# One rewrite of a two-branch kernel: u per column quarter, angle multiples by ScalarE's scale, sums in place, copies on two engines, a new written order

## The chip, the core and the metric

The kernel runs on one core of a Trainium2 chip. The core has five engines that run their own instruction streams side by side: TensorE (PE in the profile; its weight loads are shown as PEld), VectorE (DVE), ScalarE (ACT), GpSimd (POOL) and SyncE (SP), which here issues transfers. On-chip memory is SBUF (128 partitions) and PSUM, eight banks of 512 fp32 numbers per partition, into which TensorE writes. The metric is the device time of one execution in microseconds. Three runs of the kernel before gave 300.64, 302.02 and 304.17 us; the median is 302.02 us.

## What is computed

Two independent branches, of which the outputs stand side by side in the last dimension (448 + 448 columns, bf16, 2048 rows).

```python
# branch A: linear attention, 16 heads of 28, softmax feature maps
q, k, v = split(x @ wqkv)                           # x is 2048 x 448
phi(t)  = concat(softmax(t @ w_phi), softmax(-t @ w_phi))
kv, z   = phi(k)^T v, sum(phi(k))                   # per head, over all 2048 rows
o       = (phi(q) @ kv) / (phi(q) . z + 1e-6)
a       = o @ wo
# branch B: a state space layer as a long convolution, 448 channels, 256 complex states
P[d,n,l] = exp(dt[d] * A[d,n] * l)                  # l = 0..2047
K[d,l]   = Re sum_n C[d,n] * P[d,n,l] * dt[d] * B[d,n]
y        = irfft(rfft(pad(u)) * rfft(pad(K)))[:2048]
b        = y + u * Dskip
```

## The kernel before

**Branch A.** Weights are folded with `w_phi` on TensorE (`fold_weights`), x is transposed on TensorE (`flip_x`, L379), then `key_side` (L600 and around it) walks over eight pairs of row blocks: projections on TensorE, two Exp per block on ScalarE, a DMA transpose, a reciprocal (L187) and a scaled product on VectorE, and an accumulation in two PSUM banks. `query_side` does four chunks of 512 rows: projections, Exp, normalisation on VectorE, one small round trip through DRAM (`SCd`) to spread the scales over partitions, and the output projection.

**Branch B, the kernel K.** The 448 channels are done in four column quarters of 112 channels. A power P at l is split into a low factor (48 positions, tile `W`) and a high factor (16 positions, tile `U`). Per quarter, ScalarE makes the low factor's parts: `rotations` (cosine and sine of 16 multiples of an angle, tile `T`) and `dampings` (Exp of 31 multiples of a decay). In this kernel the odd multiples of angle and decay come from TensorE: `args` multiplies the high and low bf16 halves of `TH` or `AT` by identities scaled by 1, 3, ..., 15 (`PID`), four multiples to two PSUM banks, and one ScalarE instruction then covers up to four multiples, times 1, 2, 4, 8 or 16 by its scale:

```python
items += acc(psum[:, bs[e // 2], at:at + QC], [(PID[:, 4 * grp + e, :], src[:, part, cols]) for part in range(2)])
```

That is 12 ScalarE instructions for the rotations and 11 for the dampings of a quarter. VectorE multiplies the two (`damp`), extends the low factor (`far` with its inner `step`) and makes the high factor by doubling (`hi_tables`; two tiles `U` take turns). `build_k` is 448 matmuls per quarter, 16 columns of `U` against 48 of `W`, with four ScalarE copies; `scatter_k` takes the result through DRAM (`KTd`) to another layout. Since `W` is one tile, `damp` of the next quarter waits until `build_k` has read it.

**Branch B, the convolution.** It is done by matmuls with cosine tables in two halves of 1024 rows. `signal_spectrum` transforms all of u for both halves (128 matmuls of 448 columns, 16 copies on ScalarE) and writes it to DRAM (`SUd`); `conv_loads` reads it back per quarter. `kernel_spectrum_pair` transforms K of the first two quarters together, `kernel_spectrum` of each of the last two, with tables of 384 KB for each of eight frequency blocks (`load_f`, 16 transfers in all; the last two quarters share one set, held in SBUF). `conv` of a quarter is VectorE's three products of 3584 columns, one sum, one product with `Dskip`, ten smaller sums (`finish`), and 144 matmuls (`inverse`), with four copies on ScalarE and four output transfers.

**Order.** All operations are recorded in a list (`Prog.add`, L94) and issued in an order written out by hand as numbers (`ORDER`, L845); the PSUM banks are written out too (`SLOTS`). Each engine runs its own instructions strictly in that order. Nearly all VectorE work has line L162 (`tt`), ScalarE's functions have L190 (`af`), its copies L193 (`acopy`), matmuls L201, transposes L211, and transfers L216 on SP or POOL. The quarter names used below count from (0) to (3). In this order `conv` of the first quarter begins after the tables of the fourth, so that all four convolutions stand at the end.

Of the kernel before, what the change touches and what calls it, by code (L numbers as in the profile page):

```python
# [13 lines left out]
AX = mybir.AxisListType  # L14
PI = float(np.pi)

D_MODEL = 448
# [7 lines left out]
ODD = list(range(1, 16, 2))  # L25
# [9 lines left out]
SPLIT = [[(0, QC)]] * 3 + [[(0, 112), (112, 112)]]  # L35

def _round_bf16(a):
    import ml_dtypes
    return np.asarray(a, np.float32).astype(ml_dtypes.bfloat16)

# [6 lines left out]
def _dft_tables():  # L47
    m = np.arange(512) ^ 64
# [4 lines left out]
    GO = G[:, :, :, np.arange(512) ^ 64]  # L53
    GI = np.stack([GO, GO[:, :, :, ::-1]])
# [17 lines left out]
    pid = np.zeros((128, 9, 128))  # L72
    for i, p in enumerate(ODD + [-1]):
        pid[np.arange(128), i, np.arange(128)] = p
# [6 lines left out]
    return tuple(_round_bf16(t) for t in (G, GI, FT, pid, hm, hz))  # L81

class Prog:

# [9 lines left out]
    def add(self, eng, fn):  # L94
        self.ops.append((eng, fn))

    def issue(self, i):
        self.ops[i][1]()

    def run(self, order):  # L100
        assert sorted(order) == list(range(len(self.ops)))
        for i in order:
            self.issue(i)

@with_exitstack
def kernel(
# [19 lines left out]
    consts = _dft_tables()  # L126
    G_d, GI_d, F_d, P_d, M_d, Z_d = (nc.inline_tensor(t, name=f"const{i}").ap() for i, t in enumerate(consts))
    dram = ctx.enter_context(tc.tile_pool(name="dram", bufs=1, space=bass.MemoryType.DRAM))
    SUd = dram.tile([4, 128, 8, D_MODEL], BF16, name="SUd")
# [62 lines left out]
    def acopy(o, a):  # L192
        prog.add("A", lambda: nc.scalar.copy(o, a))  # L193

# [19 lines left out]
    def dma(eng, o, i):  # L214
        e = {"S": nc.sync, "AD": nc.scalar, "G": nc.gpsimd}[eng]
        prog.add(eng, lambda: e.dma_start(out=o, in_=i))  # L216

    oCB, oAT, oTH, oPW, oW, oT, oU, oTM, oSQ, oTS, oKT, oX = (
        3584, 7168, 10752, 14336, 95104, 32256, 46592, 75264, 82432, 86912, 92400, 139008)
    PID = sb(0, [128, 9, 128])  # L220
    ident = PID[:, 0, :]
    NEG = PID[:, 8, :]
    DSK = sb(2304, [128, D_MODEL])
    HM = sb(3200, [112, 4, D_HEAD + 1])
    K0 = sb(86016, [128, D_MODEL])
    bias_hp = sb(3440, [128, 1], F32)
    KVZ = sb(3456, [112, 2, 4, 4, 2])
    CB = sb(oCB, [128, 2, NCOL])
    AT = sb(oAT, [128, 2, NCOL])
    TH = sb(oTH, [128, 2, NCOL])  # L230
    PW = {k: sb(oPW + 3584 * i, [128, 2, NCOL]) for i, k in enumerate((32, 64, 128, 256, 512))}
    W = sb(oW, [128, 2, N_LO, QC])
    T = sb(oT, [128, 2, 16, QC])
    U = [sb(oU + 14336 * b, [128, N_HI, 2, QC]) for b in range(2)]
    TS = [sb(oTS + 2744 * b, [128, N_LO, 28]) for b in range(2)]
    KT = [sb(oKT + 1344 * b, [128, N_KT, 112]) for b in range(2)]

    prog.add("V", lambda: nc.vector.memset(psum[:, 4:8, 0:7 * N_LO], 0.0))
    prog.add("V", lambda: nc.vector.memset(psum[:, 0:4, 0:7 * N_LO], 0.0))
    xT = sb(oX, [112, 4, 2048])  # L240
    Wp = [sb(o, [112, 4, D_MODEL]) for o in (155392, 158976)]
    WV = sb(162560, [112, 4, D_MODEL])
    M = sb(158976, [112, 8, D_MODEL])
    wo = sb(166144, [112, 4, D_MODEL])
    G1 = sb(169728, [128, 2, 4, 512])
    raw = {nm: sb(oT + 2048 * i, [112, 4, SSM_N]) for i, nm in enumerate(("Are", "Aim", "Cre", "Bre", "Cim", "Bim"))}
    srcs = {"Are": B_A_re, "Aim": B_A_im, "Cre": B_C_re, "Bre": B_B_re, "Cim": B_C_im, "Bim": B_B_im}
    XS = [sb(o, [128, 4, D_MODEL]) for o in (oW + 10976, oW + 14560, oW + 18144, oW + 32928)]
    Wqk = sb(oW + 36512, [112, 4, 2 * D_MODEL])
    wT = sb(oTS, [112, 2, 4, D_MODEL])  # L250
    BD = sb(oTS + 7168, [112, 4, 112])
    DG = sb(oSQ + 1024, [112, 4, 112])
    DGN = sb(oSQ + 1920, [112, 4, 112])
    ldt = sb(oSQ + 2816, [4, 112])
    dtr = sb(oSQ + 3072, [4, 112])
# [10 lines left out]
    dma("S", PID, P_d)  # L266
    load_raw("Aim")
    load_x(0)
    for nm in ("Cre", "Bre", "Cim", "Bim"):
        load_raw(nm)  # L270
    for i in range(1, 4):
        load_x(i)
    dma("S", Wqk, wq3[:, :, 0:2 * D_MODEL])
    mset(BD, 0.0)
    for hh in range(4):
        dma("G", BD[28 * hh:28 * hh + 28, :, 28 * hh:28 * hh + 28], A_w_phi.rearrange("(c h) d f -> h d c f", h=4)[hh])
    prog.add("V", lambda: nc.vector.memset(bias_hp, PI / 2))

    def rep_rows(row, a):
        rs = u2.ap[0][0]  # L280
        return bass.AP(tensor=u2.tensor, offset=u2[row + 128 * (1 - a), 0].offset,
                       ap=[[2 * rs, 64], [256 * rs, 4], [1, D_MODEL]])

    def pair_rows(row, t):
        rs = u2.ap[0][0]
        return bass.AP(tensor=u2.tensor, offset=u2[row + 1023 - 128 - 256 * t, 0].offset,
                       ap=[[128 * rs, 2], [-2 * rs, 64], [1, D_MODEL]])

    ua = [sb(o, [128, 4, 2, D_MODEL]) for o in (oU, oW + 10976)]
    ab = [sb(o, [128, 2, 4, D_MODEL]) for o in (198336, oU + 14336)]  # L290

    def load_u(b):
        for a in range(2):
            dma("S", ua[b][64 * a:64 * a + 64, :, 0, :], rep_rows(1024 * b, a))
        for t in range(4):
            dma("G", ua[b][:, t, 1, :], pair_rows(1024 * b, t))

    load_u(0)
    dma("S", G1, G_d)
    dma("S", WV, wq3[:, :, 2 * D_MODEL:])  # L300

# [7 lines left out]
    def two(bs, parts=128):  # L309
        return view(psum[0:parts, bs[0], 0:1], [512 * (bs[1] - bs[0]), 2], [1, D_MODEL])  # L310
# [611 lines left out]
```

## Time and profile before

The profiled execution's span, from its first to its last instruction, is 299.6 us; the page gives no other time for that execution. The median of the three timed runs, 302.02 us, is 2.4 us above it.

| engine | busy us | share | instructions |
|---|---|---|---|
| PE matmul | 240.7 | 80% | 3877 |
| PEld | 179.8 | 60% | 3877 |
| DVE | 244.4 | 82% | 292 |
| ACT | 203.4 | 68% | 343 |
| POOL | 16.0 | 5% | 32 |

DMA moves 39.47 MB. A share of the span is a mean over stages; the stages are told apart by the windows view, which gives each engine's busy time in a stretch of the span, and by the groups of instructions kept apart by shape. An ACT instruction overlaps the one behind it, so that the busy time of a group is less than count times mean.

### The profile page before, as it was taken

How to read it: one execution, taken by the hardware profiler on the slowest of the kernel's cores; microseconds unless marked ns; L12 is line 12 of the kernel's file. 1: busy time of each engine (PE TensorE's matmuls, PEld its weight loads, DVE VectorE, ACT ScalarE, POOL GpSimd, SP SyncE). 2: the span in 40 equal slices, each digit the busy share in tenths (PEclk: the TensorE clock that was granted, in tenths of full speed). 3: DMA queues.
4: the chain of work that ended last, by engine and by line, in shares of the span. 5: the costliest groups of instructions: out<-in, count | busy, mean ns of one | idle time of the engine just before them, and what ended most of it. 6: DMA issues, size and time to landing. Idle time of an engine off the chain costs nothing. (4 is left out here: it accounts for less than half of the span.)

```text
span 299.6 us, 8829 instructions
## 1 busy us (share of the span) xinstructions
PE 240.7 (80%) x3877; PEld 179.8 (60%) x3877; DVE 244.4 (82%) x292; ACT 203.4 (68%) x343; POOL 16.0 (5%) x32
## 2 busy tenths in 40 slices
PE   1246997899469999986979996566998888999784
PEld 1245554567245567863447763466658678999784
DVE  4265995446249999997989999989899999999991
ACT  3749999599947999997199955871948611544431
POOL 8102201001000000000000001000000000000000
PEclk9999999999959999998695999777999999999999
DMA  7999387463804530045012533955879956667222
GB/s 161 239 231 194 79 246 145 64 181 67 107 10 122 122 64 4 6 136 104 3 61 58 85 79 85 331 146 109 227 255 293 301 136 176 147 184 135 46 65 63
DMA packets 65966, 39.47 MB, mean 132 GB/s; under 512 B 46616, under 2 KB 61992, under 8 KB 65544
## 3 DMA queue, kind: packets, MB, share of 16 engines
q1 hardware_dynamic: 62920, 31.57, 45.0%
q0 software_dynamic: 3008, 7.34, 8.9%
q8 instruction: 30, 0.49, 0.7%
q14 instruction: 8, 0.07, 0.1%
HBM read 26.36 MB, written 8.85 MB: 118 GB/s over the span
## 5 line engine op out<-in xcount | busy, mean ns | idle before, releaser
L201 PE MATMUL psum<-sbuf 128*16 128x48 bf16 (+9 forms) x3768 | 231.3, 258 | 39.1 <-DVE sbuf L162 11.1
L201 PEld LDWEIGHTS <-sbuf 128*16 128x16 bf16 (+4 forms) x3768 | 170.7, 109 | 98.3 <-issue 37.3
L162 DVE TENSOR_TENSOR sbuf<-sbuf 128x896 bf16<-128x896 bf16 (+13 forms) x227 | 216.7, 1002 | 12.1 <-DMA sbuf<-SCd 3.5
L193 ACT CAST sbuf<-psum 128x448 bf16<-128x448 f32 (+4 forms) x141 | 74.9, 581 | 70.6 <-PE psum L201 63.1
L190 ACT ACTIVATE sbuf<-psum 128x448 bf16<-128x448 f32 (+4 forms) x140 | 81.7, 674 | 13.2 <-DVE sbuf L162 7.5
L211 PE MATMUL psum<-sbuf 128*112 128x128 bf16 (+3 forms) x109 | 11.7, 267 | 16.2 <-DMA sbuf<-in_A_x_dram 7.2
L190 ACT ACTIVATE sbuf<-psum,sbuf 128x896 bf16<-128x896 f32 (+3 forms) x28 | 21.7, 812 | 0.0
L211 PEld LDWEIGHTS <-sbuf 128*112 128x112 bf16 (+3 forms) x109 | 10.0, 172 | 17.8 <-DMA sbuf<-in_A_x_dram 7.7
L187 DVE RECIPROCAL sbuf<-psum 128x64 bf16<-128x64 f32 x8 | 4.4, 555 | 19.4 <-PE psum L201 19.4
L190 ACT ACT_TABLE_LOAD x13 | 16.7, 1283 | 0.9 <-PEq L906 0.7
L190 ACT ACTIVATE sbuf<-sbuf 128x896 bf16<-128x896 bf16 (+3 forms) x13 | 11.6, 915 | 3.6 <-DVE sbuf L162 3.4
L180 DVE COPY sbuf<-psum 112x1024 bf16<-112x1024 bf16 (+2 forms) x16 | 7.3, 466 | 7.8 <-PE psum L211 6.6
L216 POOL DMA_DIRECT2D sbuf<-const x4 | 2.2, 556 | 126.0 <-PE psum L201 109.5
L162 DVE TENSOR_TENSOR sbuf<-psum,sbuf 128x128 f32<-128x128 f32 (+3 forms) x10 | 4.7, 491 | 3.8 <-ACT sbuf L193 3.8
L193 ACT COPY sbuf<-psum 112x896 bf16<-112x896 bf16 x5 | 4.5, 919 | 4.7 <-PE psum L211 4.7
L216 POOL DMA_DIRECT2D sbuf<-in_B_u_dram x8 | 6.6, 830 | 19.0 <-DMA sbuf<-in_B_B_re_dram 18.9
L174 DVE TENSOR_SCALAR sbuf<-sbuf 128x3584 bf16<-128x3584 bf16 (+4 forms) x11 | 6.5, 587 | 0.0
L216 POOL DMA_DIRECT2D sbuf<-SUd x4 | 2.1, 529 | 72.5 <-DVE sbuf L162 72.5
L193 ACT CAST sbuf<-sbuf 128x1792 bf16<-128x1792 f32 x3 | 5.1, 1703 | 0.0
L180 DVE COPY sbuf<-sbuf 128x448 bf16<-128x448 bf16 (+1 forms) x6 | 1.4, 238 | 3.1 <-DMA sbuf<-const 3.1
L177 DVE SCALAR_TENSOR_TENSOR sbuf<-sbuf 128x64 f32<-128x64 f32 (+1 forms) x6 | 3.0, 506 | 0.0
L196 POOL MEMSET sbuf<- 128x32 bf16 (+3 forms) x6 | 1.4, 261 | 24.7 <-PE psum L211 24.5
(12 smaller groups left out, 9.4 us busy)
## 6 DMA issues: line engine op xcount, KB each, us to landing
sbuf<-const SPq DMA_DIRECT2D x16, 384.0 KB, 3.2
SUd<-sbuf SPq DMA_DIRECT2D x8, 448.0 KB, 4.3
sbuf<-SCd SPq DMA_DIRECT2D x16, 224.0 KB
sbuf<-SUd POOLq DMA_DIRECT2D x4, 896.0 KB, 4.9
sbuf<-const POOLq DMA_DIRECT2D x2, 1024.0 KB, 7.9
sbuf<-in_A_x_dram SPq DMA_DIRECT2D x4, 448.0 KB
out_dram<-sbuf SPq DMA_DIRECT2D x4, 448.0 KB
sbuf<-in_B_u_dram SPq DMA_DIRECT2D x16, 112.0 KB, 4.0
```

Of the source, the lines that this page charges most:

```text
L162: prog.add("V", lambda: nc.vector.tensor_tensor(out=o, in0=a, in1=b, op=op))
L174: prog.add("V", lambda: nc.vector.tensor_scalar_mul(o, a, s))
L177: prog.add("V", lambda: nc.vector.scalar_tensor_tensor(out=o, in0=a, scalar=s, in1=b, op0=op0, op1=op1))
L180: prog.add("V", lambda: nc.vector.tensor_copy(o, a))
L187: prog.add("V", lambda: low(lambda: nc.vector.reciprocal(o, a)))
L190: prog.add("A", lambda: nc.scalar.activation(o, a, fn, **kw))
L193: prog.add("A", lambda: nc.scalar.copy(o, a))
L196: prog.add("G", lambda: nc.gpsimd.memset(o, v))
L201: nc.tensor.matmul(o, lhsT=l, rhs=r, **kw)
L211: nc.tensor.transpose(o, i, idn)
L216: prog.add(eng, lambda: e.dma_start(out=o, in_=i))
```

## The change

- **Angle and decay multiples.** `AT` and `TH` are kept as fp32 in SBUF; `args` and the scaled identities are gone. Each multiple is a ScalarE instruction of its own over 224 columns with the multiple as its scale: 32 per quarter for `rotations`, 31 for `dampings`.
- **u per quarter.** `signal_spectrum`, the loads of whole u and the round trip through `SUd` are gone. `u_rows` loads one quarter of u (two transfers of 224 KB), `u_spectrum` reverses the odd rows by a matmul, makes sum and difference on VectorE, transforms them (128 matmuls of 112 columns per quarter) and copies to SBUF; the product with `Dskip` is two instructions.
- **Kernel spectrum.** Each quarter for itself; the table tiles are loaded anew for each quarter (32 transfers of 384 KB) into three places.
- **Convolution.** `finish` writes its sums over the products' own tile: eight sums per quarter where there were ten.
- **Branch A.** Two row blocks share an Exp or a copy (896 or 1024 columns where there were 448 or 512).
- **Copies.** Each former copy can be on ScalarE or VectorE by a written table; 15 are on VectorE, among them four of the eight of `flip_x`, which were all there before.
- **Buffers.** One tile `U` and one `TS` (two before), a tile of its own for the dampings, two places for temporaries, two for products.
- **Order.** Written anew: the convolutions of the first two quarters stand before the end of the fourth quarter's tables, those of the last two after.

Instructions as built: TensorE 4261 matmuls and transposes and as many weight loads (3877 before), VectorE 297 (292 before), ScalarE 423 and 20 activation table loads (330 and 13 before).

```diff
-    def acopy(o, a):
-        prog.add("A", lambda: nc.scalar.copy(o, a))
+    def copy(o, a):
+        prog.either("A", lambda e: (nc.scalar.copy(o, a) if e == "A" else nc.vector.tensor_copy(o, a)))
...
+CLASSES = {
+    "T": [(117888, 7168), (125056, 7168)],
+    "C": [(137664, 7168), (144832, 7168)],
+    "F": [(166336 + 3072 * i, 3072) for i in range(3)],
+}
...
     def rotations(qt):
-        for grp in range(2):
-            p0, far_ = args(TH, qt, grp)
...
+        src = TH[:, qt * QC:(qt + 1) * QC]
+        for r, p in enumerate(LO_ABS):
+            af(T[:, 0, r, :], src, ACT.Sin, scale=float(p), bias=bias_hp)
+            af(T[:, 1, r, :], src, ACT.Sin, scale=float(p))

     def dampings(qt):
...
+        src = AT[:, qt * QC:(qt + 1) * QC]
+        for r in range(31):
+            af(A[:, r, :], src, ACT.Exp, scale=float(LO[r]))
...
+    def u_rows(qt):
+        for r in range(2):
+            dma("S", UA[qt][:, r].rearrange("p b t x -> p (b t) x"), ...)
+
+    def u_spectrum(qt):
+        ua, su, AB, RV = UA[qt], SU[qt], AB_[qt], RV_[qt]
+        bs = prog.take("P", 0, 1)
+        mms([(psum[:, bs[b], 0:D_MODEL], REV, ua[:, 1, b].rearrange("p t x -> p (t x)"), dict(start=True, stop=True))
+             for b in range(2)])
+        copy(RV.rearrange("p b t x -> p b (t x)"), two(bs))
+        add(AB[:, :, 0], ua[:, 0], RV[:, :, ::-1, :])
+        sub(AB[:, :, 1], ua[:, 0], RV[:, :, ::-1, :])
+        for b in range(2):
+            for cp in range(2):
+                bs = prog.take("P", *((0, 1), (2, 3))[cp])
+                for st in range(2):
+                    mms([it for mt in range(4) for it in acc(
+                        psum[:, bs[st], 112 * mt:112 * mt + 112],
+                        [(GS[0][:, cp, jt, 128 * mt:128 * mt + 128], AB[:, b, cp ^ st, jt, :]) for jt in range(4)])])
+                copy(su[:, b, cp].rearrange("p s m x -> p s (m x)"), two(bs))
...
+    def kernel_spectrum(qt):
+        sk, kt_ = SK[qt % 2], KT[qt % 2]
+        for mp in range(4):
+            fts = []
+            for k in range(2):
+                ft = sb(FP[prog.take("F", (2 * mp + k) % 3)[0]], [128, 2, 6, 128])
+                dma("S", ft, F_d[2 * mp + k])
...
         def finish(b, t):
-            y = Y[:, b]
+            y, S = t[:, 0], t[:, 1].rearrange("p r (c x) -> p r c x", c=2)
             sub(y[:, 0], t[:, 0, 0], t[:, 1, 1])
             add(y[:, 1], t[:, 0, 1], t[:, 1, 0])
-            S = S_[:, b]
             add(S[:, 0], y[:, :, 0:448], y[:, :, 448:896])
-            sub(S[:, 1, 0], y[:, 0, 0:448], y[:, 0, 448:896])
-            sub(S[:, 1, 1], y[:, 1, 448:896], y[:, 1, 0:448])
+            sub(S[:, 1], view(y[:, 0, 0:1], [1344, 2], [1, 448]), view(y[:, 0, 448:449], [448, 2], [1, 448]))
...
     rotations(0)
     hi_tables(0)
     dampings(0)
...
+    u_rows(0)
+    u_spectrum(0)
+    kernel_spectrum(0)
+    tables(1, ALL)
+    scatter_k(1)
     rotations(2)
     hi_tables(2)
+    conv(0)
+    u_rows(1)
+    u_spectrum(1)
+    kernel_spectrum(1)
     dampings(2)
...
+    dampings(3)
+    tables(3, SPL)
+    scatter_k(3)
+    conv(2)
+    u_rows(3)
+    u_spectrum(3)
+    kernel_spectrum(3)
+    conv(3)
```

## The prediction, made before the result was known

> **What bounds the kernel now.** First the page's busy times with the 40 slices:
>
> ```profile
> PE 240.7 (80%) x3877; PEld 179.8 (60%) x3877; DVE 244.4 (82%) x292; ACT 203.4 (68%) x343; POOL 16.0 (5%) x32
> ...
> DVE  4265995446249999997989999989899999999991
> ACT  3749999599947999997199955871948611544431
> ```
>
> VectorE is full from the twelfth slice on, ScalarE ahead of that. The windows view puts numbers to the stages (columns: stretch, length, busy time of PE, PEld, DVE, ACT, POOL, granted clock, DMA share, GB/s):
>
> ```profile
> 0.00:32.00 32.00, 13.34 (x104) 10.67 (x105) 16.32 (x19) 20.61 (x23) 10.36 (x19) 1.00 0.94 199
> 32.00:88.00 56.00, 45.68 (x405) 28.74 (x403) 31.88 (x40) 49.66 (x76) 2.51 (x7) 0.95 0.56 117
> 88.00:137.00 49.00, 46.95 (x765) 32.21 (x764) 47.81 (x55) 43.90 (x71) 0.00 (x0) 0.98 0.33 77
> 137.00:238.40 101.40, 82.03 (x1394) 58.42 (x1393) 94.52 (x123) 68.88 (x131) 1.59 (x3) 0.88 0.54 154
> 238.40:296.10 57.70, 52.67 (x1216) 49.74 (x1214) 53.86 (x60) 19.84 (x43) 1.59 (x3) 1.00 0.52 122
> ```
>
> Until 32 us the loads set the pace (DMA share 0.94). From 32 to 88 ScalarE is busy 49.7 of 56 us and VectorE only 31.9. At 88 the first `damp` starts, since the first quarter's rotations and dampings end at 86; from there VectorE is full: 47.8 of 49 us, then 94.5 of 101.4, then 53.9 of 57.7. At 238.4 the last table operation of the fourth quarter ends, and the four convolutions fill VectorE and TensorE to the end. So two things set the time: when ScalarE lets VectorE start, and VectorE's sum after that. VectorE's idle time is 55 us, 40 of it ahead of 88. Durations come from the groups kept apart by shape:
>
> ```profile
> L190 ACT ACTIVATE sbuf<-psum 128x896 bf16<-128x896 f32 x36 | 32.4, 949 | 0.2 <-PE psum L201 0.2
> L190 ACT ACTIVATE sbuf<-psum 128x224 bf16<-128x224 f32 x20 | 7.6, 408 | 0.0
> L190 ACT ACTIVATE sbuf<-psum,sbuf 128x224 bf16<-128x224 f32 x8 | 3.5, 454 | 0.0
> L190 ACT ACT_TABLE_LOAD x13 | 16.7, 1283 | 0.9 <-PEq L906 0.7
> L162 DVE TENSOR_TENSOR sbuf<-sbuf 128x896 bf16<-128x896 bf16 x58 | 34.6, 619 | 0.9
> L201 PE MATMUL psum<-sbuf 128*128 128x112 bf16 x824 | 42.5, 213 | 4.5 <-DVE sbuf L162 3.8 <-ACT sbuf L193 0.6
> ```
>
> and the steps from start to start from ScalarE's timeline:
>
> ```profile
> 110.36 0.36 ACT L190 ACTIVATE sbuf<-psum 128x224 bf16<-128x224 f32 x1
> 110.61 0.44 ACT L190 ACTIVATE sbuf<-psum,sbuf 128x224 bf16<-128x224 f32 x1
> 110.94 0.91 ACT L193 CAST sbuf<-psum 128x896 bf16<-128x896 f32 x1
> ```
>
> A 224-column instruction is followed 0.25 us later by the next, one with a bias column (the cosines) 0.33 us later.
>
> **The change, part by part.** Steps are start to start.
>
> *Angle multiples.* No row has 224 columns from SBUF. At 896 columns two instructions from SBUF last 1.83 us (mean 0.961), so 0.87 start to start; two from PSUM last 1.73 (mean 0.949), so 0.78 to 0.80. SBUF costs some 0.06 more: I take 0.29 without bias and 0.385 with it; the low bound is PSUM's 0.25 and 0.33, the high one the full durations, 0.41 and 0.45. A quarter is 16 x 0.385 + 47 x 0.29 = 19.8 us; before, rotations ran from 159.0 to 166.4 and dampings took 6.4, together 13.8. So +6 per quarter, +24 on ScalarE. TensorE loses the 128 `args` matmuls, 15.6 us by their stages, which were not at its limit.
>
> *Table loads* go from 13 to 20: 7 x 1.29 = +9 on ScalarE. The row shows no idle time around them (0.9 us for 13). The Trainium skill, in "ScalarE: Activation LUTs", section "What ACT_TABLE_LOAD costs", counts a drain of about 1.38 us beside each load, 2.66 together, and a rule there says to finish one set before the other; by it the seven would cost 19 us and the total would be some 10 us longer, but the timeline has a load from 157.73 to 159.01 and the next instruction at 159.03, so the row stands.
>
> *Copies and merging.* Four of `flip_x` come to ScalarE (+3.6), the reversed u adds four of 896 columns (+3.2); seven copies of 896, one of 336 and three fp32 casts leave (6.0 and 4.8), merged branch A instructions save 2.6, the spectrum copies 1. With the two terms above ScalarE gets +25: 203 becomes 229.
>
> *VectorE.* Off: four flips (2.7 by 0.678), two subtractions of `AT`/`TH` (2.2), 16 sums of 448 columns against 8 of 896 (-0.5). On: seven copies near 0.55 to 1.0, three casts and one small copy (8.8 bounded by the 0.678 and 1.087 rows of PSUM reads); u's sums and `Dskip` are equal within 0.6. Sum +5: 249.5.
>
> *TensorE.* u's 512 matmuls of 112 columns at 0.0515 (42.5/824) are 26.4 against 24.7; TensorE ends near 228.
>
> **The sum, in three legs.** The order as built is read by what each engine has issued at two cuts.
>
> Cut 1 is the end of the third quarter's rotations and dampings on ScalarE, ahead of the third `damp`. ScalarE has there 139 x 0.29 + 46 x 0.385 = 58.0; 23 copies of 896 at 0.8 = 18.4; 16 Exp of 1024 at 0.9 = 14.4; 16 of 896 at 0.8 = 12.8; 16 others of 896 from SBUF 14.2; eleven copies 6.0; two squares 3.2; 16 table loads 20.6; together 147.6. VectorE has 125 by then, so ScalarE leads here. It begins at 6.4 us (A's states, as before) with 1.6 already done: 152.4 without a wait. Before, between 32 and 137, ScalarE lacked 11.4 of 105 us (waits for PE's results); with the same share cut 1 is at 170. The single activations wait for nothing but `TH` and `AT` and stand between the waiting copies, so I take half the share: 146.0/0.945 + 6.4 = 161.
>
> Cut 2 is the last table operation of the fourth quarter. VectorE has between the cuts the tables of two quarters (31.6 and 33.2 by the rows of before), one chunk's query products 2.4, u's sums 3.9 and two convolutions without their `Dskip` product (2 x 12.3): 95.7. At densities seen before, 0.932 to 0.976, that is 98 to 103; I take 99.7. So 261, against 238.4.
>
> The tail after cut 2 was 61.2 us. Now two convolutions are left: 29.5 us of VectorE, but TensorE has half a `build_k` 5.5, u's two spectra 14.0, K's spectrum 6.2 and four inverses 14.8, 40.5 in all, and a chain: half `build_k` 5.5; `KTd` out and back 0.5 + 2.8 + 4.0, hidden but for 1 under u's spectrum 7.0; K's spectrum, u's last spectrum and half an inverse pair, 16.9, so 30; copy 0.55, two products 4.0, four sums 2.2; a third product, the sum and four sums 6.2; inverse 3.7; copy and output 3.5 (296.1 to 299.6 before). That is 50; 47 if the first product starts before K's last block, 57 if the tables' transfers hold it up.
>
> 161 + 99.7 + 49.5 = 310 of span, against 299.6. With the 2.4 us between span and median: **312 us**. The bounds of the legs give 152.4 + 98 + 47 + 2.4 = 300 and 170 + 103 + 57 + 2.4 = 332.
>
> *Covers and new waits.* With one `U`, `hi_tables` of a quarter waits for the `build_k` before it; behind it on VectorE stands everything, among it the `damp` that needs ScalarE anyway; I price it in the density (11 us of `build_k` uncovered would be the loss per quarter). u's loads and spectra of the first two quarters lie under VectorE's tables; uncovered, 7 each. `u_rows` is issued early on SP; K's table tiles now queue on SP with K's scatter and the outputs, and a tile waiting for one of three places holds what is behind it.
>
> **Rivals.**
> *Faster.* If 224 columns from SBUF run at PSUM's step, cut 1's sum falls by 139 x 0.04 + 46 x 0.055 = 8, and if ScalarE's waits vanish too, the time is 144.4 + 98 + 47 + 2.4 = 292; half of both gives 300. For it speaks that the first big `damp` product needs only 54.4 us of ScalarE's work, some 62 to 66 us after the start against 88 now, that 40 of VectorE's 55 idle us lie there, and that the front loads about 4.4 MB without u and its table. Against it: the gain is used up as ScalarE, with 79 us of work per 80 of VectorE's until cut 1, gives VectorE no lead. It decides from a ScalarE wait share under 3% on.
> *Same.* 299 to 305, the two halves meeting.
> *Slower by the tables' transfers.* Before, eight tiles through four places took 223.9 to 240.8 with 12.4 us of matmuls; 4.5 us were lost at 281 GB/s. Four times through three places, the last one bare: +5 to +9, 317 to 321.
> *Not what it says.* Only 15 of the copies can be on VectorE, so ScalarE isn't relieved by that; this is in the sum already.
>
> **How the numbers follow.** Forecast (305 to 317) 0.44; slower by transfers (above) 0.13; same (299 to 305) 0.15; faster (under 299) 0.28. A measurement of this kernel tells about 1% from no change. The range 293 to 324 leaves out a part of the faster cases and the sum of all the high ends, 2 in 10 together at most.
>
> **What would show it.** The groups: 124 `Exp` and 128 `Sin` of 224 columns at 0.29 and 0.385 per step, 20 table loads. The first 128x6720 product on VectorE near 64 to 70, ScalarE busy over 90% to about 160, VectorE's idle time in 100 to 160 put down to ACT L199, the last table sums near 261, a last stretch of 50 us in which TensorE is busier than VectorE. Wrong it is if the ScalarE step is near 0.25, if the stretch to cut 1 has VectorE full, or if the tail has PE waiting for `const` transfers for over 5 us.

## The result, and the profile after

The changed kernel takes **326.25 us** (median of five runs, 321.13 to 328.30) against 302.52 us for the kernel before on the same chip (300.64 to 304.38): a ratio of **1.069, with a 95% interval of 1.058 to 1.080**. (An execution can fall into a faster or a slower state, and ratios here compare executions in the faster one alone, two of these five; the medians' own ratio is 1.078.) It is slower, as forecast, but by 24 us where 10 were forecast; 326 lies above the range's upper end of 324. The profiled execution is the shortest of the five: span 319.4 us, time 321.13.

The page of the changed kernel, its busy times and 40 slices, and the shares of the chain that ended last:

```profile
PE 242.4 (76%) x4261; PEld 189.4 (59%) x4261; DVE 246.8 (77%) x297; ACT 225.8 (71%) x443; POOL 6.4 (2%) x18
...
DVE  4699988599646989796379997969699594279690
...
ACT  2989999899997979999992798884243334355521
...
PE 30%; DMA 24%; DVE 11%; ACT 5%; SPq 4%; issue 3%; DVEq 0%
```

VectorE no longer has a row of nines: it is fuller early and has holes from the eleventh slice to the end. The last line is the chain; 24% of the span in it are DMA. It can't be compared with the kernel before, whose chain could be followed over 19% of the span only (DVE 16%, all behind 238 us). The windows view of the changed kernel, cut where the forecast cut it (stretch, length, busy time of PE, PEld, DVE, ACT, POOL, granted clock, DMA share, GB/s):

```profile
0.00:88.00 88.00, 56.85 (x581) 37.85 (x585) 72.36 (x77) 77.36 (x147) 6.43 (x18) 0.88 0.47 99
88.00:170.30 82.30, 66.46 (x1196) 44.37 (x1184) 60.10 (x93) 75.45 (x148) 0.00 (x0) 0.92 0.38 88
170.30:266.80 96.50, 77.26 (x1574) 67.53 (x1575) 84.58 (x97) 53.19 (x116) 0.00 (x0) 0.88 0.48 138
266.80:319.40 52.60, 41.86 (x928) 39.60 (x925) 29.71 (x33) 19.76 (x33) 0.00 (x0) 1.00 0.48 117
```

170.3 is the start of the third big product of `damp`, 266.8 the end of the last table operation. The same view of the kernel before, cut at the time of its own last table operation (238.4) and at the same 88 and 170.3:

```profile
0.00:88.00 88.00, 59.02 (x507) 39.41 (x508) 48.20 (x58) 70.27 (x98) 12.87 (x26) 0.97 0.70 147
88.00:170.30 82.30, 74.53 (x1229) 50.41 (x1231) 77.41 (x97) 68.98 (x111) 0.00 (x0) 0.91 0.30 70
170.30:238.40 68.10, 54.45 (x940) 40.23 (x930) 64.91 (x81) 43.80 (x91) 1.59 (x3) 0.92 0.68 200
238.40:299.60 61.20, 52.67 (x1216) 49.74 (x1214) 53.86 (x60) 20.37 (x44) 1.59 (x3) 1.00 0.51 118
```

Length less VectorE's busy time is its idle time. It was 39.8, 4.9, 3.2 and 7.3 us in the four stretches; now it is 15.6, 22.2, 11.9 and 22.9. So the early start of `damp` brings 24.2 us, and the three later stretches lose 17.3, 8.7 and 15.6. With 2.4 us more work that is 19.8, the whole difference of the spans. At 88 us VectorE is 24 us of work ahead of the kernel before (72.4 against 48.2), at 170.3 only 7 (132.5 against 125.6): **the gain was had, and given back behind 88 us.**

What VectorE waits for in the changed kernel (engine, line and releaser: us in total, times, longest):

```profile
DVE sbuf L171 <- ACT sbuf L202: 12.1, 5, 3.4
DVE sbuf L171 <- DMA sbuf<-in_B_u_dram: 11.7, 3, 7.8
DVE sbuf L196 <- PE psum L210: 10.7, 5, 4.4
DVE sbuf L171 <- DMA sbuf<-SCd: 9.7, 4, 4.3
```

Here L171 are VectorE's sums and products, L196 its reciprocals, L202 the copies, L210 the matmuls. Four causes of nearly one size, two of them transfers; before, u and `SCd` together were 6.4 us. TensorE has a transfer at the head of its list too, the table tiles of the kernel's spectra:

```profile
PE psum L210 <- DMA sbuf<-const: 15.4, 9, 3.7
```

13.6 of the 15.4 us lie between 170.3 and 266.8. But a list of waits doesn't tell which of them the time would be without, and ScalarE, 62.4 of 67.3 us busy from 103 to 170.3, was the cause that the forecast had named. That is what the experiments were for.

### The profile page after: what moved, and what is told of

Its sections match the earlier page's. It is cut to its first block, busy times and chain, and to the rows that moved or that the text cites. A ratio compares the mean times of both kernels' runs of the same rounds, so it can differ in the third digit from the quotient of the medians.

```text
span 319.4 us, 9636 instructions
## 1 busy us (share of the span) xinstructions
PE 242.4 (76%) x4261; PEld 189.4 (59%) x4261; DVE 246.8 (77%) x297; ACT 225.8 (71%) x443; POOL 6.4 (2%) x18
## 2 busy tenths in 40 slices
DMA packets 60322, 35.37 MB, mean 111 GB/s; under 512 B 44888, under 2 KB 55272, under 8 KB 60024
## 4 chain that ended last, share of the span: by engine, by line
PE 30%; DMA 24%; DVE 11%; ACT 5%; SPq 4%; issue 3%; DVEq 0%
PE psum L210 30%; DVE sbuf L171 11%; DMA sbuf<-const 9%; DMA sbuf<-SCd 7%; SPq L225 4%; DMA sbuf<-sbuf 3%; ACT sbuf L199 3%; DMA sbuf<-KTd 2%; ACT sbuf L202 2%; DMA sbuf<-in_B_u_dram 1%; DMA SCd<-sbuf 1%; DMA KTd<-sbuf 1%; DVE sbuf L183 0%; DVE sbuf L189 0%; DVE sbuf L196 0%
## 5 line engine op out<-in xcount | busy, mean ns | idle before, releaser
L210 PE MATMUL psum<-sbuf 128*16 128x48 bf16 (+7 forms) x4152 | 235.1, 252 | 66.1 <-DMA sbuf<-const 15.4
L210 PEld LDWEIGHTS <-sbuf 128*128 128x128 bf16 (+4 forms) x4152 | 182.2, 111 | 116.9 <-issue 45.4
L171 DVE TENSOR_TENSOR sbuf<-sbuf 128x896 bf16<-128x896 bf16 (+14 forms) x227 | 214.0, 1001 | 38.5 <-ACT sbuf L202 12.1
L202 ACT CAST sbuf<-psum 128x448 bf16<-128x448 f32 (+3 forms) x106 | 68.5, 681 | 76.7 <-PE psum L210 69.2
L199 ACT ACTIVATE sbuf<-sbuf 128x224 bf16<-128x224 f32 (+5 forms) x277 | 106.3, 461 | 2.4 <-DVE sbuf L171 1.6
L199 ACT ACTIVATE sbuf<-psum 128x896 bf16<-128x896 f32 (+1 forms) x32 | 29.8, 972 | 3.4 <-issue 3.0
L199 ACT ACT_TABLE_LOAD x20 | 25.7, 1283 | 0.9 <-PEq L831 0.7
L196 DVE RECIPROCAL sbuf<-psum 128x64 bf16<-128x64 f32 x8 | 4.4, 555 | 10.7 <-PE psum L210 10.7
L202 ACT COPY sbuf<-psum 112x1024 bf16<-112x1024 bf16 (+2 forms) x8 | 7.8, 976 | 6.5 <-PE psum L210 5.2
L202 DVE COPY sbuf<-psum 112x1024 bf16<-112x1024 bf16 (+2 forms) x7 | 5.0, 722 | 1.2 <-PE psum L210 1.2
L202 DVE CAST sbuf<-psum 128x896 bf16<-128x896 f32 (+2 forms) x5 | 4.8, 969 | 1.0 <-PE psum L210 1.0
L171 DVE TENSOR_TENSOR sbuf<-psum,sbuf 128x128 f32<-128x128 f32 (+2 forms) x8 | 2.6, 341 | 1.2 <-PE psum L210 1.2
L202 DVE CAST sbuf<-sbuf 128x1792 bf16<-128x1792 f32 x3 | 3.2, 1084 | 0.0
L196 DVE RECIPROCAL sbuf<-sbuf 128x64 f32<-128x64 f32 x4 | 2.2, 550 | 0.1
```

Of the source, the lines that this page charges most:

```text
L171: prog.add("V", lambda: nc.vector.tensor_tensor(out=o, in0=a, in1=b, op=op))
L196: prog.add("V", lambda: low(lambda: nc.vector.reciprocal(o, a)))
L199: prog.add("A", lambda: nc.scalar.activation(o, a, fn, **kw))
L202: prog.either("A", lambda e: (nc.scalar.copy(o, a) if e == "A" else nc.vector.tensor_copy(o, a)))
L210: nc.tensor.matmul(o, lhsT=l, rhs=r, **kw)
```

## The experiments

Each group ran on one chip together with the kernel before; ratios are to that kernel, with 95% intervals. The changed kernel itself was run again in the second group (f1, 1.085), and gains below are counted from there. In the first group its ratio was 1.069, so up to 5 us of any gain can be the base's: f2 doesn't clear that, e1 barely does, f4 (17 us) and i1 (21 us) do. Theories at the start: **S**, ScalarE's work up to the third quarter's dampings sets the first cut (the forecast's); **T**, the transfers that now stand between producers and users set it; **O**, the written order makes the waits, whatever the operations cost.

### Taking ScalarE's work or the transfers away

```diff
 # e1, in kernel_spectrum (e3 = e1 and e2)
-                dma("S", ft, F_d[2 * mp + k])
+                if qt == 0:
+                    dma("S", ft, F_d[2 * mp + k])
 # e2, in dampings
-            af(A[:, r, :], src, ACT.Exp, scale=float(LO[r]))
+            if qt == 0:
+                af(A[:, r, :], src, ACT.Exp, scale=float(LO[r]))
 # e4, in rotations, both lines
-            af(T[:, 1, r, :], src, ACT.Sin, scale=float(p))
+            af(T[:, 1, r, :], src, ACT.Exp, scale=float(p) / 256)
```

> The changed kernel with K's table tiles transferred for the first quarter only: 24 of 32 transfers of 384 KB are left out, and the later quarters multiply by whatever lies in the three places (their spectra are not the right ones). Theory S (ScalarE's added work sets when the third quarter can start, 168 us, and the rest follows): under 4 us faster than the changed kernel's 326, since ScalarE's last third-quarter rotation stays at 168. Theory T (TensorE waits in its fixed order for these tiles, 15.4 us in the waits of the changed kernel, and they slow the other transfers): 10 to 16 us faster, all of it after 175 us.

> The changed kernel with the dampings computed for the first quarter only and used for all four (93 ACTIVATEs of 224 columns and, as built, 10 of 20 table loads are left out of ScalarE: 93 x 0.29 + 10 x 1.29 = 40 us, some 26 of them ahead of the third quarter's last rotation). Theory S: that rotation moves from 168 to 142 to 152, and the time falls by 12 to 25 us. Theory T: under 5 us. A third theory O (neither: the written order with single buffers makes each engine wait for the others in turn, and VectorE, 77% busy, and TensorE, 76%, follow one another): the rotation moves, the end moves by less than half as much.

> Both together (the same two parts left out). S: as with the dampings alone, within 3 us. T: as with the transfers alone, within 4 us. If the two causes stand one behind the other (front and second half), the gains add to 20 to 35 us. O: under 15 us in all.

> The changed kernel with the rotations' function replaced by the exponential at a scaled-down angle (its T values are not cosines and sines): the same instructions, but 7 table loads where there are 20. S with a price of 1.29 us per load: 13 loads are 16.8 us of ScalarE, some 12 ahead of 168 us, and the time falls by 6 to 12 us; if a switch costs twice that, by 15 to 25. T and O: under 5 us.

> The changed kernel itself, as the base for the runs beside it: 321 to 328 us, as before; if its time moves by more than 1% the runs on other chips can be compared by their ratios only.

| run | median us | ratio to before |
|---|---|---|
| f1, the changed kernel again | 325.32 | 1.085 (1.073 to 1.098) |
| e1, table tiles once | 319.36 | 1.060 (1.047 to 1.073) |
| e2, dampings once | 325.07 | 1.082 (1.068 to 1.096) |
| e3, both | 317.90 (312.42 to 318.69) | no interval |
| e4, 7 table loads instead of 20 | 326.95 | 1.091 (1.082 to 1.100) |

**S falls, in this order.** With the dampings of three quarters gone, ScalarE does 187 us instead of 226 and the time stays. The windows view of f1 and then of e2, 103 to 168 us:

```profile
103.00:168.00 65.00, 53.60 (x759) 32.92 (x757) 51.58 (x78) 61.86 (x113) 0.00 (x0) 0.92 0.40 91
```

```profile
103.00:168.00 65.00, 52.31 (x750) 32.72 (x749) 50.13 (x77) 45.52 (x75) 0.00 (x0) 0.89 0.35 79
```

ScalarE loses 16 us of work there, and VectorE does not do more in the same time. The third `damp` product starts at 174.2 (169.8 in f1). What grows instead is ScalarE's wait for matmul results; the line of waits in f1 and in e2:

```profile
ACT sbuf L202 <- PE psum L210: 83.2, 37, 6.4
```

```profile
ACT sbuf L202 <- PE psum L210: 109.6, 44, 7.2
```

The single activations had filled the time between copies that were waiting anyway. ScalarE was full without being late. Nor did the cut move: the last rotation of the third quarter ends at 173.2 in e2 and at 169.2 in f1. The same follows for the table loads: thirteen fewer (e4) bring nothing.

**T holds in part.** e1 gains 6 to 8 us: 7.6 by the ratios against f1, where the intervals just touch, and 5.7 by the medians against e2 in its own group, where they overlap. T had asked for 10 to 16 and S for under 4, so it is neither's forecast. e3 lies 1.5 us below e1: the dampings add nothing there either.

### More transfers taken away

```diff
 # f2, SCd read and written for the first chunk only
-        dma("S", SCd[sc], SCT)
+        dma("S", SCd[sc], SCT) if sc == 0 else prog.add("S", lambda: None)
 # f3, build_k reads a tile of its own, so that hi_tables needn't wait for it
+    UC = sb(14400, [128, N_HI, 2, QC])
...
-                                      U[:, :, ri, 112 * c + x], W[:, ri, :, 112 * c + x],
+                                      UC[:, :, ri, 112 * c + x], W[:, ri, :, 112 * c + x],
 # f4 = e1, f2, f3, and u loaded for two quarters only; g3 = f2 and e2; g4 = f4 and e2
+            if qt in (0, 3):
+                dma("S", UA[qt][:, r].rearrange("p b t x -> p (b t) x"), ...)
```

In f2 the reads of `SCd` into `SB` are left out for the later chunks as well.

> The changed kernel with the round trip of the attention's scales through DRAM (one write of 32 KB and four reads of 224 KB per chunk) made for the first chunk only; the other three chunks multiply by the first one's scales. The runs before showed that neither ScalarE's load nor the tables' transfers alone set the time. Theory Q (VectorE, in its written order, stands behind these round trips: 9.7 us in its waits, and 7% of the chain): the third quarter's big damp product moves from 170 to 158 to 163 us and the time falls by 6 to 12 us. Theory B (single buffers: hi_tables waits until build_k has read U, u's load until the convolution has read the one tile of u): under 3 us. Theory S (ScalarE, busy 62 of 67 us in that stretch): under 3 us.

> The changed kernel with build_k reading the tables of powers in place of U (its K is not the right one; same matmuls): hi_tables of a quarter need not wait for build_k of the quarter before it. Theory B: VectorE's waits ahead of hi_tables (3.2 us at 101, 1.5 at 160, 0.9 at 214) go, and the time falls by 4 to 8 us. Theory Q and S: under 2 us, since what is behind waits again at the next point.

> Four parts left out together: the scales' round trip after the first chunk, u's loads of the second and third quarter, K's table tiles after the first quarter, and build_k's wait on U (the values are those of other quarters or chunks). Theory O (the engines wait on one another in turn, through transfers and single buffers): 25 to 40 us faster than the changed kernel, below the kernel before. Theory S (ScalarE sets the front): the third quarter's last rotation stays within 5 us of 168, and the time falls by 10 to 16 us, all after it.

> The changed kernel with the scales' round trip for the first chunk only and the dampings for the first quarter only. Each alone gave little (4 us, and under 1). If the two are side by side in the stretch from 100 to 170 us, so that either one alone holds the third quarter's damp product, both together move it from 170 to 150 to 158, and the time falls by 10 to 16 us. If something else holds it (TensorE's order, the attention's products), the gain is 4 to 6 us, the sum of the two.

> The changed kernel with the transfers and waits of the run without transfers left out (scales, u, K's tables, U) and the dampings once as well. Without transfers it took 17 us less than the changed kernel and stayed 7 above the one before. If ScalarE is what was left, another 8 to 15 us go, to 294 to 300. If it is the order in which TensorE and VectorE hand work to each other, under 4 us go.

| run | median us | ratio to before |
|---|---|---|
| f2, `SCd` once | 321.25 | 1.074 (1.064 to 1.084) |
| f3, `U` free | 324.36 | 1.086 (1.074 to 1.097) |
| f4, tables, `SCd`, u and `U` | 308.53 | 1.030 (1.018 to 1.041) |
| g3, `SCd` and dampings once | 317.20 | 1.054 (1.043 to 1.065) |
| g4, f4 and dampings once | 303.19 | 1.012 (1.006 to 1.017) |

f3 shows no cost of the single `U` (its interval is 1 point wide to each side). f2 brings 3.5 us by the ratios, less than the 6 to 12 expected, with overlapping intervals; the third `damp` product starts at 165.2 instead of 169.8, not at 158 to 163. Single profiles differ by some us in their front, so it is better counted from the first `damp` product: the third comes 100.9 to 104.1 us later in the four profiles without the `SCd` trips (f2, f4, g3, g4) and 105.8 to 109.7 in the seven with them, whether the dampings are there or not.

f4 brings 17 us, 5.6 of the 8.5 points: **most of the loss is time in which an engine stands before a transfer.** Its third product is hardly sooner (168.5, behind a first one that is 2.4 us later than in f1), and the gain lies behind: from there to the last table operation 91.4 us instead of 98.6 in f1, then 50.3 instead of 56.6. That is under the 25 to 40 that O had asked for. Once transfers are gone ScalarE's work counts again: by the ratios g4 is 5 us below f4 (the intervals just miss each other), and g3 6 below f2 (they overlap). Both lie between what their rivals had asked for. Behind one wait stands the next.

### One part of the change put into the kernel before

```diff
 # g1: AT and TH kept as fp32, no args, one activation for each multiple
-            p0, far_ = args(TH, qt, grp)
+            args(TH, qt, grp)          # issues nothing now
...
-                    af(dst, src, ACT.Sin, scale=float(f), **(dict(bias=bias_hp) if c_ == 0 else {}))
+                    each(ACT.Sin, [(T[:, c_, r0 + e * (1 if n == 4 else step), :], src,
+                                    dict(scale=float(f * ODD[4 * grp + e]), **kw)) for e in range(n)])
 # g2: fourteen copies on VectorE
+    ON_V = {57, 70, 74, 111, 113, 116, 118, 121, 123, 126, 128, 141, 143, 153}
...
+        if len(prog.ops) in ON_V:
+            prog.add("V", lambda: nc.vector.tensor_copy(o, a))
```

> The kernel before with one part of the change alone: its angle and decay multiples by ScalarE's scale (63 ACTIVATEs of 224 columns per quarter in place of 23 larger ones and 32 matmuls, AT and TH kept in fp32), in its own order and with its 13 table loads. By the prediction's step ScalarE gets 6 us per quarter: the first damp product waits for ScalarE alone in that kernel (88 us), so the first quarter's 6 us are lost in full and of the others, which lie under VectorE's work, 0 to 3 us: 6 to 9 us slower than the kernel before, 306 to 310. If only the written order of the changed kernel made it slow (theory O), this part costs under 3 us.

> The kernel before with 14 of ScalarE's copies (11 of u's spectrum, three of 1792 columns) on VectorE, all of them ahead of the first damp product: 13.6 us less of ScalarE, 14 more of VectorE, which has 40 us without work there. If ScalarE sets the start of that product at 88, it moves to 76 to 82, and the time falls by 5 to 10 us, below both kernels. If the attention's chain (transposing transfers, reciprocals) sets it, under 2 us.

g1 takes 310.34 us, 1.033 (1.024 to 1.042); g2 takes 312.68, 1.042 (1.032 to 1.052). In the old order the activations do cost, 9 us (6 to 9 were expected), but not where I had put it: the first `damp` product starts at 89.3 (89.1 before), the second at 135.7 (133.5), the third at 182.6 (176.7), the fourth at 224.2 (216.9), and the last table operation ends at 246.8 (238.4). It is the later quarters in which VectorE, full until then, catches up with ScalarE:

```profile
DVE sbuf L174 <- ACT sbuf L448: 6.3, 3, 3.6
```

g2 moves copies off ScalarE in the stretch where it was the fullest and VectorE had 24 us to spare, 32 to 88 us. The windows view of g2:

```profile
32.00:88.00 56.00, 45.48 (x362) 27.37 (x361) 45.00 (x52) 29.77 (x52) 2.51 (x7) 0.94 0.44 106
```

ScalarE falls from 49.7 to 29.8 us there, and yet the first `damp` product moves from 89.1 to 100.4. That is neither of the two outcomes expected. The last reciprocal ahead of that product, for which VectorE stands 8.4 us for TensorE, starts at 85.2 in the kernel before; the line of g2 below it has the same wait and starts at 96.5:

```profile
85.22 0.56 DVE L187 RECIPROCAL sbuf<-psum 128x64 bf16<-128x64 f32 x1 [8.38 <-PE psum L201]
```

```profile
96.50 0.56 DVE L187 RECIPROCAL sbuf<-psum 128x64 bf16<-128x64 f32 x1 [8.54 <-PE psum L206]
```

VectorE's free time was waiting time, and the copies came on top of it. Which of the fourteen does it was not tried.

### The same operations in another order

What was left was to change nothing but `ORDER`. New orders were made by replaying recorded durations and moving operations, with every two operations that share a buffer kept in their order. In h transfers were taken to run side by side, in i as queuing behind one another. j1 started from the durations of i1 and has a copy table of its own besides, with 16 copies on VectorE, and 16 table loads.

```diff
 ORDER = [int(i) for i in (
...
-    "14 123 72 125 133 116 43 44 105 55 88 121 136 86 41 58 137 18 12 118 93 20 69 70 112 119 47 45 21 50 60 19 89 "
+    "20 40 39 124 44 123 87 72 85 19 41 131 55 21 43 45 140 69 60 73 88 18 58 137 93 86 106 125 91 117 138 89 59 "
...
```

> The changed kernel with all its operations, buffers, transfers and PSUM banks as they are (22 table loads), only the written order of its 1209 operations is another one, found by moving operations while every pair that shares a buffer keeps its order. Theory O (the written order makes VectorE, TensorE and ScalarE wait for one another in turn, and that is where the time went): 20 us faster or more than the changed kernel, 285 to 305. Theory M (more work: ScalarE's 22 us, the transfers, the smaller buffers set the time whatever the order): within 6 us of 325.

> The kernel before with another written order, found in the same way (nothing else is changed). Its VectorE is 95% busy after 88 us, so only the front has something to give, 55 us of idle VectorE in all: 285 to 297, 2 to 5% faster. If the changed kernel reordered comes to the same time as this one or less, the change's parts cost little by themselves and its order cost nearly all; if it stays 9 us above it or more, the parts cost what the run of the scale multiples alone showed.

> The changed kernel with a third written order, found with transfers that queue behind one another (the order of the run before took 7 us off, with TensorE and VectorE waiting for the scales' reads and the table tiles longer than was assumed for it). Nothing else differs. Theory O (order): 10 us or more below the changed kernel's 325, and at or below the first reordering's 318. Theory M (the parts' work sets the time whatever the order): no lower than 318.

> The kernel before with another order found in the same way; the first such order made it 10 us slower. If the written order of the kernel before is fitted to the chip as it is, this one is slower again, 303 to 313. If its front can be made denser, 288 to 298.

> The changed kernel in a fourth order, found from the durations of the run with the third one; four of its copies have changed engines (16 on VectorE where there were 15), and as built there are 16 table loads. Theory O: 296 to 302, level with the kernel before or a little below it. If the parts of the change cost something that no order hides, it stays 2 to 4 us above the kernel before, as the third order did (1.5%).

> The changed kernel in the third order (304.5 us) with the dampings computed for the first quarter only (93 ACTIVATEs and 10 of 20 table loads left out, 40 us of ScalarE; the other quarters use the first one's). In the changed kernel's own order this moved nothing. If ScalarE's added work is what keeps the third order above the kernel before, the time falls by 5 us or more, below the kernel before. If it is hidden in that order too, under 3 us.

| run | median us | ratio to before |
|---|---|---|
| h1, changed kernel reordered | 317.90 | 1.061 (1.047 to 1.074) |
| h2, kernel before reordered | 313.46 | 1.042 (1.032 to 1.052) |
| **i1, changed kernel reordered** | **304.52** | **1.015 (1.009 to 1.021)** |
| i2, kernel before reordered | 311.05 | 1.033 (1.024 to 1.042) |
| j1, from i1's durations | 310.75 | 1.025 (1.019 to 1.031) |
| j2, i1 with dampings once | 304.77 | 1.004 (0.998 to 1.009) |

i1 has the operations, buffers, transfers (35.37 MB) and 20 table loads of the changed kernel, and takes back 7.1 points of f1's 8.5: **21 us by the order alone** (16 if counted from the first group's 1.069). Its windows:

```profile
0.00:88.00 88.00, 60.33 (x733) 42.31 (x733) 72.86 (x79) 80.22 (x154) 6.38 (x18) 0.86 0.50 104
88.00:170.30 82.30, 66.20 (x1068) 43.00 (x1069) 67.04 (x94) 72.24 (x146) 0.00 (x0) 0.92 0.42 102
170.30:249.70 79.40, 70.03 (x1554) 63.06 (x1554) 77.86 (x93) 53.70 (x115) 0.00 (x0) 0.94 0.54 152
249.70:302.70 53.00, 42.78 (x910) 40.70 (x907) 29.41 (x33) 18.96 (x31) 0.00 (x0) 0.95 0.45 109
```

VectorE has done the same work at the last table operation (217.8 us, 217.0 in the changed kernel) and is there 17 us sooner. Seven of them come from the second stretch and ten from the third, in which it is now busy 77.9 of 79.4 us. The first stretch and the tail bring nothing: VectorE's idle time is 15.1 us in the one (15.6 in the changed kernel) and 23.6 in the other (22.9). Four waits in the whole span:

| wait, us in total | changed kernel | i1 |
|---|---|---|
| VectorE for `SCd` | 9.7 | 0.3 |
| VectorE for u | 11.7 | 2.5 |
| VectorE's reciprocals (L196) for TensorE | 10.7 | 3.7 |
| TensorE (L210) for table tiles | 15.4 | 0.5 |

Not all of this is gain. The gain of the second stretch is `SCd`, all of whose 9.7 us lay there, less what other waits grew by. In the third stretch VectorE waited 8.1 us for ScalarE's copies and 2.6 for u, the copies waited 39.6 us for TensorE (16.7 in i1), and TensorE 13.6 us for table tiles; in i1 VectorE's two waits there are 0.3 us together and TensorE's is 0.5. But 7.4 of the 10.7 us ahead of reciprocals lay before 88 us, where i1 has other waits in their place, and 9.1 of u's 11.7 lay in the tail.

The lines themselves, from the timeline of VectorE in the changed kernel (start, length, engine, operation, what it had idled for): the four products of the query side and the first work behind the tables,

```profile
120.27 2.63 DVE L171 TENSOR_TENSOR sbuf<-sbuf 112x2048 bf16<-112x2048 bf16 x3 [1.44 <-DMA sbuf<-SCd]
131.65 8.77 DVE L171 TENSOR_TENSOR sbuf<-sbuf 112x2048 bf16<-112x2048 bf16 x7 [2.21 <-DMA sbuf<-SCd]
156.19 2.36 DVE L171 TENSOR_TENSOR sbuf<-sbuf 112x2048 bf16<-112x2048 bf16 x2 [4.35 <-DMA sbuf<-SCd]
168.02 2.36 DVE L171 TENSOR_TENSOR sbuf<-sbuf 112x2048 bf16<-112x2048 bf16 x2 [1.66 <-DMA sbuf<-SCd]
...
274.68 2.35 DVE L171 TENSOR_TENSOR sbuf<-sbuf 128x896 bf16<-128x896 bf16 x4 [7.84 <-DMA sbuf<-in_B_u_dram]
```

and SP's timeline there, which issues the transfer that the last line waits for:

```profile
256.37 0.99 SPq L225 DMA_DIRECT2D out_dram<-sbuf  x2
266.83 0.38 SPq L225 DMA_DIRECT2D sbuf<-in_B_u_dram  x1
...
268.97 0.45 SPq L225 DMA_DIRECT2D sbuf<-in_B_u_dram  x1
```

SP stands from 257.4 to 266.8 for a result of TensorE (its longest wait of that kind, 9.4 us), and VectorE, whose tables end at 266.8, has nothing but this quarter of u to go on with. In i1 the two transfers are issued at 248.8 and 250.6, around the end of its tables (249.7), and the wait is still there under other names: TensorE's first matmul on u waits for the transfer, ScalarE's copy for that matmul, and VectorE 6.6 us for the copy. The lines of SP, TensorE, ScalarE and VectorE in i1:

```profile
248.84 2.15 SPq L225 DMA_DIRECT2D sbuf<-in_B_u_dram  x2
```

```profile
254.82 2.04 PE L210 MATMUL psum<-sbuf 128*128 128x448 bf16 x66 [0.66 <-DMA sbuf<-in_B_u_dram]
```

```profile
255.39 2.43 ACT L202 CAST sbuf<-psum 128x896 bf16<-128x896 f32 x4 [3.79 <-PE psum L210]
```

```profile
256.33 2.23 DVE L171 TENSOR_TENSOR sbuf<-sbuf 128x896 bf16<-128x896 bf16 x4 [6.63 <-ACT sbuf L202]
```

So T and O are one answer as far as the last table operation: another order hides the transfers there that the order of the changed kernel puts close before their users. The late transfer of u isn't hidden in either, and the tail is 53.0 us in i1, 52.6 in the changed kernel.

Hiding transfers is not enough by itself. h1 was to be 20 us faster by O or within 6 by M, and is 7 faster: VectorE's waits for `SCd` and u are 1.3 and 1.5 us there and TensorE's for table tiles 7.6, but from 88 to 170.3 VectorE still idles 17.7 us (i1 15.3, the changed kernel 22.2), 5.9 of it ahead of reciprocals that wait for TensorE. j1, expected at 296 to 302, is a miss too: 310.75 us. Its transfers are as well hidden (`SCd` 2.0 us), but its reciprocals wait 12.7 us for TensorE, 5.3 of them between 88 and 170.3; the replay that proposed it did not foresee these. h2 was to speed up the kernel before and made it slower by 4%; i2, for which both had been named, is slower by 3%. No better order was found for that kernel. j2 lies a point (3 us) below i1 by the ratios, with intervals that just overlap, and level with it by the medians. So the dampings cost less than the 5 us that would have made them the reason, and whether they cost 3 or nothing in that order stays open. No version here beats that kernel.

## Why the prediction was wrong

The direction was right, the size was not. By its own steps, in spans: cut 1 was put at 161 and came at 168.4 (last rotation on ScalarE); the leg to cut 2 was put at 99.7 and took 98.4; the tail was put at 49.5 and took 52.6. That is 319.4 against 310. The median lies a further 5.1 us above this execution, the shortest of five. In f1, which lies near the median (span 324.9), the three legs are 169.2, 99.2 and 56.5: cut 1 and the tail are off by 7 to 8 us each.

- **Angle multiples: right.** Counted from start to start, rotations and dampings take 80.2 us of ScalarE over four quarters, 20.1 each, forecast 19.8. As single durations they overlap:

```profile
L199 ACT ACTIVATE sbuf<-sbuf 128x224 bf16<-128x224 f32 x252 | 85.5, 414 | 0.4 <-DVE sbuf L171 0.2
```

- **Table loads: right.** Twenty, 25.7 us, hardly any idle time with them:

```profile
L199 ACT ACT_TABLE_LOAD x20 | 25.7, 1283 | 0.9 <-PEq L831 0.7
```

The Trainium skill's 2.66 us for a switch ("ScalarE: Activation LUTs", "What ACT_TABLE_LOAD costs") is not what this row shows: 1.28 us each. And by e4 not even these set the time in this kernel.
- **First product of `damp`: nearly right.** It starts at 62.4, forecast 64 to 70. But the reading of the kernel before that stood behind it, that ScalarE's rotations and dampings let VectorE start at 88, does not hold: VectorE's long wait there is for TensorE, ahead of the last reciprocal (8.4 us, above), and g1, in which ScalarE does 74.0 us of work ahead of 88 instead of 70.3, still starts that product at 89.3.
- **ScalarE's and VectorE's sums: right**, 225.8 for 229 and 246.8 for 249.5. **TensorE's was mis-sized:** 242.4 for 228. u's spectra take 30.4 us, forecast 26.4, and K's 31.1 against 24.7 before, at a granted clock of 0.909 (0.949 before). It isn't where the time went: i1 has 239.3 us of it and is 21 us faster.
- **Cut 1: the failed step is "so ScalarE leads here".** ScalarE's work and its idle time to that cut were near the forecast (152.8 and 15.6 us, 147.6 and 13.4), but e2 shows that the cut doesn't move when the work goes. The sign named for it, VectorE's idle time in 100 to 160 put down to ScalarE's activations, failed as well: 0.5 us are, and 8.0 are put down to `SCd`. In order, VectorE waits 9.7 us for `SCd` between 118 and 168; the step that priced what lies beside what never named this round trip. Without three quarters of it the third product comes some 5 us sooner after the first (the profiles above), which is most of the 7 that the cut was late. What holds it besides was not isolated.
- **The cover of u: failed.** "u's loads and spectra of the first two quarters lie under VectorE's tables": 2.6 us of them do not, and the last two quarters' loads, which I did not price at all, cost VectorE 9.1 behind cut 2 (8.6 in f1).
- **"Densities seen before": failed.** The leg came out right by luck, by two errors that cancel. VectorE did 86.5 us of work there and not 95.7 (5.6 us more was done ahead of cut 1, and the whole is smaller); its density was 0.88, not 0.932 to 0.976, and from 88 to 170.3 it was 0.73. A density belongs to an order and not to an engine: i1 has 0.98 from 170.3 to its last table operation.
- **The tail: right in kind, too short.** TensorE is busy 41.9 of its 52.6 us, VectorE 29.7 (forecast 40.5 and 29.5); what the sum lacked is the wait for u.
- **The rival "slower by the tables' transfers"**, at +5 to +9, agrees with what e1 gains, 6 to 8, as far as that is clear of noise. I weighed it as instead of the forecast, while it came on top, as did `SCd` and u. The rival "faster" hung on ScalarE's step and waits; even with three quarters of its dampings gone (e2) nothing is gained.

What stays open: the last 1.5% between i1 and the kernel before, and how the 21 us divide among the waits. f2 and e1 give 3.5 and 6 to 8 for two of them one at a time, neither clear of noise by itself; u's transfers alone and the reciprocals alone were not tried.

## What to carry to other kernels

A busy share on an engine that runs strictly in order is not its pace: 93% busy ScalarE was filling gaps, and taking 39 us of its work away moved nothing until the transfers were gone too. When a change comes with a new written order, price that order by the distance between each transfer's issue and its user, for every transfer on the path, and not by the densities of the old order. To tell an order's cost from its operations' cost, change the order alone; here that was worth 16 to 21 us, more than any one part that was left out. And when a wait has vanished from the list, look whether the same engine idles at the same place for another releaser, as VectorE does in i1 behind the tables.

## What the runs showed of the hardware that I had not expected

- Fourteen copies moved from the fullest engine of a stretch to one that idled 24 of its 56 us made the kernel 11.6 us slower (g2).
- In the changed kernel the reads of `SCd` (four of 224 KB) let VectorE go 5.1 to 6.0 us after the end of their last issue, the late u transfer of 224 KB 5.3 us after its own. A transfer issued when its user is ready cost about that here.
- The granted clock is lower in the changed kernel (0.909, 0.877 to 0.911 over its runs, against 0.949) with nearly the same TensorE time. i1 has 0.913 and is 21 us faster, and one execution of the kernel before took 297.98 us at 0.924, so the clock is not the cause here.
